# Decode step of attention and MLP, gated: two weight loads merged, the bias loaded once, the last accumulator begun four rows earlier

## The chip, the cores and the metric

The kernel runs on one core of a Trainium2 chip. The metric is the device time of one execution in microseconds (us), the median of several runs. Engines are named as in the profile: PE is TensorE's matmul, PEld its weight load, DVE is VectorE, ACT ScalarE, POOL GpSimd, SP SyncE; SPq and ACTq are the sequencers of SP and ACT, which issue the DMAs.

## The reference, cut to what matters

```python
# x [2, 1, 576], k_cache and v_cache [2, 32, 4096, 128], wq [576, 4096], wo [4096, 576],
# w1 [576, 4608], b1 [4608], w2 [4608, 576], b2 [576], gate_w [576], all float32
g = sigmoid((x * gate_w).sum(-1, keepdims=True))
q = (x @ wq).reshape(B, 1, 32, 128).transpose(0, 2, 1, 3)
p = softmax(einsum("bhqd,bhkd->bhqk", q, k_cache) * 128 ** -0.5)
a = einsum("bhqk,bhkd->bhqd", p, v_cache).transpose(0, 2, 1, 3).reshape(B, 1, 4096) @ wo
b = gelu(x @ w1 + b1) @ w2 + b2
out = g * a + (1 - g) * b
```

## The kernel before

**The ring.** One tile `ring` of 128 partitions holds everything that is loaded: three slots of 16384 floats a partition. At first wq and w1 lie in it, with small temporaries behind them (`temp`). Then 16 units pass through it, each four heads of one batch row: a K load and a V load of 8.39 MB, one slot each. Then come three last loads (`LAST`, L66 to L70), into the slots of the last-but-one V, the last K and the last V: w2's rows 0 to 27 (a "row" is one of the 36 rows of 576 floats that each partition holds), in two transfers; then w2's rows 28 to 35, a second copy of half of w2's last row spread over 16 partitions in four small transfers (`wx`), and wo's rows 0 to 15, in two transfers; then wo's rows 16 to 31, in pieces of 7, 4, 3 and 1 rows, the last row once more in three pieces. `load_last` (L143) issues these on SP, in this order; SP works through its queue in order. `load_next` (L200) issues the next load when the slot that it goes to has been named free; the instruction itself then waits for the readers of the part that it overwrites. A load also waits for an older transfer which used the same semaphore, since there are eight semaphores that are used in turn.

**The start.** `b1r` is set to zero by POOL (L210). `load_b1` (L215) puts b1 into four partitions, one in each group of 32, row 0 of the group, on ACT's queue; x and gate_w follow (L223, L224). POOL and DVE make an identity and constants (`pick` L252, `xe` L259, `xT` L272, `g1z` L372 are zeroed by DVE and then partly filled by it). PE forms x's transposes, the gate (L279) and x @ wq (`qps`, L303); ACT copies the result (L313), issues the load of b2 (L314) and, in five pieces, a second load of b1 into row 1 of each group (L315, issued at L218), and scales q (L330). `q_unit` (L343) spreads q over the partitions for four units: a multiplication on POOL (L347), a matmul (L351), a copy on ACT (L353). `acc_mm` (L363) adds a product of two rows (the two batch rows) to the accumulator `acc` in PSUM, in halves of 288 columns at one of four places; the first such product (L367) is b2's, with `g1z`. Then x @ w1 (`hps`), the addition of `b1r` (L390), a transposition (L395) and the gelu (L396 to L405), whose result times 1 - g is `hg`.

**The units.** For each unit i: `softmax` of unit i-1 (ACT, L531), then DVE multiplies K by q (L506), POOL and DVE sum over 128 (L510 to L512), DVE finds the maximum (L516 to L525); PE multiplies the probabilities of unit i-1 with V (`av`, L545).

**The end.** The order is written out by hand (L604 to L623):

```python
    softmax(k)
    mlp_out(0, 14)
    av(k)
    load_next(("v", k))
    assert not seq
    keep(k // 2)
    mlp_out(14, 18)
```

`mlp_out(lo, hi)` (L421) adds hg times w2's rows to `acc`. `keep` and `combine` (L556, L562) gather the attention's output, `norm_sum`, `norm_t` and `o_turn` (L570 to L436) divide and turn it into `oP`; between them stand further parts of `mlp_out` and `mlp_x`. `wo_out(0, FOLD)` (L438) adds oP times wo's rows below FOLD to `acc`. `last_out` (L443) copies `acc` to SBUF on ACT (L446), and gathers wo's rows from FOLD on in a second accumulator `res`, in four pieces of 144 columns a row (`part`, L457); behind the first of these rows, four matmuls with the matrix `fold` (L467) add the four places of `acc` to it. Row 31 comes in two parts, as its pieces land (L457, then L481); DVE and ACT copy the output in two steps each (L477, L486), and SP writes it (L487).

Of the kernel before, what the change touches and what calls it, by code (L numbers as in the profile page):

```python
# [12 lines left out]
P = 128  # L13
# [6 lines left out]
def kernel(  # L20
# [14 lines left out]
    nc = tc.nc  # L35
    B, H, SK, DH = k_cache.shape
# [13 lines left out]
    NG = 4  # L50
# [3 lines left out]
    F4 = F // NG  # L54
# [3 lines left out]
    NF = F // P  # L58
# [5 lines left out]
    SLOTS = 3  # L64

    LAST = (  # L66
        (("w2", 0, 14), ("w2", 14, 28)),
        (("w2", 28, 36), ("wx", 0, 1), ("wo", 0, 8), ("wo", 8, 16)),
        (("wo", 16, 23), ("wo", 23, 27), ("wo", 27, 30), ("wo", 30, 31), ("wo", 31, 32)),
    )  # L70
    FOLD = 27
    SLOT = R * DH
    ALIGN = 512
    FREE0 = 16512
# [96 lines left out]
    def temp(n, parts=P):  # L171
        t = ring[:parts, used["t"]:used["t"] + n]
        used["t"] += n
        assert used["t"] <= SLOTS * SLOT
        return t

    def late(n, parts=P):
        t = ring[:parts, used["e"]:used["e"] + n]
        used["e"] += n
        assert not seq and used["e"] <= used["z"]  # L180
        return t
# [18 lines left out]
    def load_next(what):  # L200

        free.add(what)
        while seq and held[-SLOTS] in free:
            load()
# [3 lines left out]
    b1r = temp(F4)  # L208
# [3 lines left out]
    load()  # L212
    load()

    def load_b1(b, ends):  # L215
        to, src = b1r.rearrange("(g q) n -> g q n", g=NG)[:, b], b1.rearrange("(g n) -> g n", g=NG)
        for u, v in zip(ends, ends[1:]):
            nc.scalar.dma_start(to[:, u:v], src[:, u:v])  # L218


    load_b1(0, (0, F4))
    for b in range(B):
        nc.scalar.dma_start(xg[b:b + 1], x[b])  # L223
    nc.scalar.dma_start(xg[B:B + 1], gate_w[None, :])  # L224
# [24 lines left out]
    selr = cp.tile([P, RB], F32, name="selr")  # L249
    nc.vector.tensor_reduce(selr, sel.rearrange("p j e r -> p r j e"), AX.XY, ALU.add)  # L250
    pick = cp.tile([P, 2 * NO - G], F32, name="pick")
    nc.vector.memset(pick, 0.0)  # L252
    nc.vector.tensor_reduce(pick[:, NO - G:NO], sel.rearrange("p j e r -> p e j r"), AX.XY, ALU.add)

    xe = temp(2 * P, B + 1).rearrange("p (e c) -> p e c", e=2)
    nc.vector.memset(xe, 0.0)  # L259
    for e in range(2):  # L260
        nc.vector.tensor_copy(xe[:, e, e::2], xg[:, NX * P:])  # L261
    def x_rows(rows):
# [6 lines left out]
    for c, src in enumerate(srcx):  # L269
        nc.tensor.transpose(xps[:, c, :B + 1], src, ident[:B + 1, :B + 1])  # L270
    xT = temp(NXT * 32).rearrange("p (c b) -> p c b", b=32)
    nc.vector.memset(xT, 0.0)  # L272
    nc.vector.tensor_copy(xT[:, :, :B], xps[:, :, :B])
    gT = temp(NX + 1)
    nc.vector.tensor_copy(gT, xps[:, :NX + 1, B])
# [36 lines left out]
    for m, ps in enumerate(qps):  # L312
        nc.scalar.copy(qrow[:, m * 512:(m + 1) * 512], ps)  # L313
    nc.scalar.dma_start(b2r, b2[None, :])  # L314
    load_b1(1, (0, 232, 464, 696, 928, F4))  # L315

    to = temp(HG * NO).rearrange("p (f o) -> p f o", f=HG)
# [43 lines left out]
    def acc_mm(lhsT, rhs, k, start=False, stop=False, lo=0):  # L363
        m = lhsT.shape[-1]
        for s in range(lo, lo + rhs.shape[-1] // DS):
            o = 64 * (k % 2) + 32 * s
            nc.tensor.matmul(  # L367
                acc[o:o + m], lhsT, rhs[:, (s - lo) * DS:(s - lo + 1) * DS], start=start, stop=stop, skip_group_check=True
            )

    g1z = cp.tile([1, 2, 32], F32, name="g1z")
    nc.vector.memset(g1z, 0.0)  # L372
    nc.vector.tensor_copy(g1z[:, 0, :B], g1[0:1])
    for k in range(2):
        acc_mm(g1z[:, k], b2r, k, start=True)
# [17 lines left out]

    ht = temp(F4).rearrange("p (r c) -> p r c", c=32)
    nc.vector.transpose(ht, hrow.rearrange("q (p r) -> q r p", r=NF))  # L395
    hb = ht[:, :, :B]  # L396
    hg = cp.tile([P, NF, B], F32, name="hg")
    t = temp(NF * B).rearrange("p (r b) -> p r b", b=B)
    nc.vector.tensor_mul(t, hb, hb)
# [21 lines left out]
    def mlp_out(lo, hi):  # L421
        for r in range(lo, hi):
            acc_mm(hg[:, r], rows["w2", r], r)
# [14 lines left out]
    def wo_out(lo, hi):  # L438
        for r in range(lo, hi):
            acc_mm(oP[:, :, r], rows["wo", r], r)  # L440


    def last_out():  # L443
        res = ps_big.tile([32 * (NC - 1) + B, DO], F32, tag="big", name="res")
        sums = late(DS)
        nc.scalar.copy(sums, acc)  # L446

        def half(t, s):
            if s < 2:
                return t[:, s * DO:(s + 1) * DO]  # L450
            return t.rearrange("p (q g c) -> p g q c", q=2, g=2)[:, s - 2]

        def cols(row, s):
            return half(row[:, s // 2 * DS:(s // 2 + 1) * DS], s)

        def part(r, s):
            nc.tensor.matmul(  # L457
                res[32 * s:32 * s + B], oP[:, :, r], cols(rows["wo", r], s),
                start=r == FOLD, stop=r == 31, skip_group_check=True,
            )  # L460

        for r in range(FOLD, 31):
            for s in range(NC):
                part(r, s)
            if r == FOLD:
                for s in range(NC):
                    nc.tensor.matmul(  # L467
                        res[32 * s:32 * s + B], fold[:, s // 2], half(sums, s),
                        start=False, stop=False, skip_group_check=True,
                    )  # L470

        osb = late(D, B)
        cpy = (nc.vector.tensor_copy, nc.scalar.copy)
        for s in range(2):
            part(31, s)
        for s in range(2):
            cpy[s](osb[:, s * DO:(s + 1) * DO], res[32 * s:32 * s + B])  # L477
        DW = DO // 2
        for q in range(2):
            for s in range(2, NC):  # L480
                nc.tensor.matmul(  # L481
                    res[32 * s:32 * s + B, q * DW:(q + 1) * DW], oP[:, :, 31], cols(rows["wo", 31], s)[:, q],
                    start=False, stop=True, skip_group_check=True,
                )
        for s in range(2, NC):
            cpy[s - 2](cols(osb, s), res[32 * s:32 * s + B].rearrange("p (q c) -> p q c", q=2))  # L486
        nc.sync.dma_start(out.rearrange("b s d -> (b s) d"), osb)  # L487
# [39 lines left out]
    def softmax(i):  # L527
        p = pt[i % NPB][:, EB:].rearrange("p (t c) -> p t c", c=32)
        for e in range(E):
            w = slice(e * PE_, (e + 1) * PE_)  # L530
            nc.scalar.activation(  # L531
                p[w, :, e * RB:(e + 1) * RB], st[i][w].rearrange("p (t c) -> p t c", c=RB), AF.Exp,
                bias=bias[i][w], accum_out=rs[w, i * E + e:i * E + e + 1],
            )


    def av(i):
        half = i % 2
        if half == 0:
            avs[i // 2] = ps_av.tile([P, 512], F32, tag="av", name=f"av{i // 2}")  # L540
        ps = avs[i // 2]
        p = pt[i % NPB]
        for t in range(NT):
            j = t % 4
            nc.tensor.matmul(  # L545
                ps[32 * j:32 * j + 32],
                p[:, 32 * t + EB * (1 - half):32 * t + EB * (1 - half) + 32],
                vt[i][:, RB * t:RB * (t + 1)].rearrange("p r d -> p (r d)"),
                start=(half == 0 and t < 4),
                stop=(half == 1 and t >= NT - 4),  # L550
            )


    def keep(i):
        t = ep.tile([P, RB, DH], F32, tag="avs", name=f"avs{i}")
        nc.vector.tensor_mul(  # L556
            t, avs[i].rearrange("p (r d) -> p r d", d=DH), selr.unsqueeze(2).to_broadcast([P, RB, DH])
        )
        avs[i] = t
# [43 lines left out]

    k = N - 1  # L604
    softmax(k)
    mlp_out(0, 14)
    av(k)
    load_next(("v", k))
    assert not seq
    keep(k // 2)  # L610
    mlp_out(14, 18)
    combine(k // 2)
# [8 lines left out]
    mlp_out(28, NF)  # L621
    wo_out(0, FOLD)
    last_out()  # L623


# [26 lines left out]
```

## Time and profile before

| | |
|---|---|
| time, median of 3 runs | 722.4 us (722.3 to 722.56) |
| the profiled execution: time | 722.53 us |
| the profiled execution: span | 720.5 us |
| busy: DVE, PE, POOL, ACT | 71%, 30%, 20%, 5% |
| loaded, mean rate over the span | 308.84 MB, 429 GB/s |

The span runs from the first to the last instruction of the program; the time holds some 2 us more. An engine's busy time is the sum of its instructions; DMA share is the mean busy share of the 16 DMA engines. A timeline row reads: start, duration, engine, line, operation, out<-in, shapes, count, and in brackets the idle time before and what ended it. A row of the chain of waits reads: start, duration, what. A row of a table of stretches has the length, the busy time of PE, PEld, DVE, ACT and POOL with their counts, the granted TensorE clock (1.00 is full), DMA share and GB/s.

### The profile page before, as it was taken

To read this page: it belongs to the slowest core of one execution; us is meant where nothing else is said; L and a number is where in the kernel's file an instruction comes from. 1 tells how busy PE (TensorE), PEld (TensorE's weight loads), DVE (VectorE), ACT (ScalarE), POOL (GpSimd) and SP (SyncE) were. 2 spreads that over 40 slices of the span, in tenths; PEclk is the share of its full clock that TensorE was granted. 3 is DMA by queue.
4 is the path that set the end of the run, shared out by engine and by line. 5 is a ranking of instruction groups with operands and counts; after the bars stand their busy time and mean duration, and the time that the engine had idled before them with its cause. 6 is when DMAs were issued, how large, how long until landed. Compare 5 with 4: busy or idle time off the path is not lost.

```text
span 720.5 us, 3849 instructions
## 1 busy us (share of the span) xinstructions
PE 213.3 (30%) x1631; PEld 61.1 (8%) x1631; DVE 513.9 (71%) x154; ACT 38.0 (5%) x142; POOL 144.2 (20%) x31
## 2 busy tenths in 40 slices
PE   0781022140514050504133140405060503123295
PEld 0330000010101010101000000101010101000031
DVE  0104969789695969596969879696959695978810
ACT  0010010100001010101010100001010101010100
POOL 1000130404050404022140404040503022040400
PEclk9996557565757575666656575757575665657598
DMA  9999999999999999999999999999999999999996
GB/s 409 411 446 430 426 444 415 458 416 451 422 448 427 440 426 433 434 426 440 429 438 437 437 437 433 438 426 429 440 427 437 433 438 433 440 429 441 414 421 289
DMA packets 7276, 308.84 MB, mean 429 GB/s; under 512 B 830, under 2 KB 1362, under 8 KB 1628
## 3 DMA queue, kind: packets, MB, share of 16 engines
q1 hardware_dynamic: 7204, 308.55, 99.1%
q8 instruction: 13, 0.21, 0.1%
q10 hardware_dynamic: 56, 0.05, 0.0%
q14 instruction: 3, 0.02, 0.0%
HBM read 308.59 MB, written 0.00 MB: 428 GB/s over the span
## 4 chain that ended last, share of the span: by engine, by line
DMA 49%; DVE 35%; PE 13%; ACT 2%; issue 1%; ACTq 0%; POOL 0%; DVEq 0%; SPq 0%; POOLq 0%
DMA ring<-in_A_k_cache_dram 40%; DVE ring L506 19%; DVE s L511 10%; PE av L545 9%; DVE s L512 5%; DMA ring<-in_A_wo_dram 3%; DMA ring<-in_gate_w_dram 3%; ACT p L531 2%; DMA ring<-in_B_w_dram 2%; PE hps L303 2%; PE qps L303 2%; DMA ring<-in_B_b_dram 1%; PE zps L279 0%; DVE ring L395 0%; DVE m L516 0%
## 5 line engine op out<-in xcount | busy, mean ns | idle before, releaser
L506 DVE TENSOR_TENSOR ring<-ring,q 128x16384 f32<-128x16384 f32 x16 | 275.6, 17225 | 116.4 <-DMA ring<-in_A_k_cache_dram 116.4
L510 POOL TENSOR_TENSOR ring<-ring 128x3968 f32<-128x3968 f32 x16 | 137.0, 8564 | 494.7 <-DVE ring L506 494.7
L545 PE MATMUL av<-ring,p 128*32 128x512 f32 x1024 | 138.1, 700 | 174.6 <-ACT p L531 174.6
L511 DVE TENSOR_REDUCE s<-ring 128x66 f32<-128x8448 f32 x16 | 143.2, 8953 | 1.3
L562 PE MATMUL oall<-avs,pick 128*64 128x512 f32 x16 | 14.8, 1028 | 197.0 <-DVE avs L556 169.4
L512 DVE TENSOR_REDUCE s<-ring 128x62 f32<-128x3968 f32 x16 | 68.4, 4276 | 0.0
L545 PEld LDWEIGHTS av<-ring,p 128*32 128x32 f32 x1024 | 35.3, 127 | 282.9 <-issue 218.5
L531 ACT ACTIVATE p<-s,bs 32x128 f32<-32x128 f32 x64 | 25.5, 398 | 486.1 <-DVE bs L525 484.9
L351 PE MATMUL qb<-qm,spread 64*128 64x512 f32 x8 | 7.3, 1013 | 73.2 <-POOL qm L347 73.2
L390 DVE TENSOR_TENSOR ring<-hps,ring 128x384 f32<-128x384 f32 x3 | 1.7, 559 | 26.3 <-PE hps L303 26.1
L562 PEld LDWEIGHTS oall<-avs,pick 128*64 128x64 f32 x16 | 2.2, 196 | 203.9 <-DVE avs L556 203.9
L367 PE MATMUL acc<-ring,hg 128*2 128x288 f32 x142 | 11.0, 457 | 25.4 <-DMA ring<-in_B_w_dram 25.4
L261 DVE COPY ring<-ring 3x64 f32<-3x64 f32 x2 | 0.3, 182 | 19.6 <-DMA ring<-in_gate_w_dram 19.6
L477 DVE COPY ring<-res 2x144 f32<-2x144 f32 x1 | 0.3, 297 | 17.7 <-PE res L481 17.7
L556 DVE TENSOR_TENSOR avs<-av,selr 128x512 f32<-128x512 f32 x8 | 5.5, 682 | 9.9 <-PE av L545 9.9
L531 ACT ACTIVATION_READ_ACCUMULATOR p<-s,bs 32x1 f32 x64 | 11.8, 184 | 0.0
L347 POOL TENSOR_TENSOR qm<-qall,mine 64x512 f32<-64x512 f32 x4 | 4.1, 1033 | 37.5 <-ACT qall L330 37.5
L303 PE MATMUL hps<-ring 128*32 128x384 f32 x120 | 11.5, 548 | 0.0
L367 PE MATMUL acc<-ring,oP 128*2 128x288 f32 x108 | 10.1, 505 | 4.6 <-DMA ring<-in_A_wo_dram 4.6
L303 PE MATMUL qps<-ring 128*32 128x512 f32 x80 | 11.0, 712 | 0.0
L351 PEld LDWEIGHTS qb<-qm,spread 64*128 64x128 f32 x8 | 1.8, 277 | 76.1 <-POOL qm L347 76.1
L270 PE MATMUL xps<-ident,ring 3*128 3x3 f32 x10 | 1.3, 250 | 23.0 <-DMA ring<-in_gate_w_dram 23.0
(87 smaller groups left out, 65.1 us busy)
## 6 DMA issues: line engine op xcount, KB each, us to landing
ring<-in_B_w_dram SPq DMA_DIRECT2D x2, 4608.0 KB, 34.3
ring<-in_B_w_dram SPq DMA_DIRECT2D x2, 4032.0 KB
ring<-in_A_wo_dram SPq DMA_DIRECT2D x2, 2304.0 KB, 15.2
ring<-in_B_w_dram SPq DMA_DIRECT2D x1, 2160.0 KB
ring<-in_A_wo_dram SPq DMA_DIRECT2D x1, 2016.0 KB
ring<-in_B_w_dram SPq DMA_DIRECT2D x1, 1152.0 KB, 14.6
ring<-in_A_wo_dram SPq DMA_DIRECT2D x1, 1152.0 KB
ring<-in_A_wq_dram SPq DMA_DIRECT2D x1, 1024.0 KB
```

Of the source, the lines that this page charges most:

```text
L303: nc.tensor.matmul(ps[32 * j:32 * j + 32, :width], lhs, ts[c][:, o:o + width], start=(k == 0), stop=last, skip_group_check=True,)
L347: nc.gpsimd.tensor_mul(t, qall.unsqueeze(1).to_broadcast([NO, NQ, DH]), mine[:, u[0]:u[-1] + 1].unsqueeze(2).to_broadcast([NO, NQ, DH]),)
L351: nc.tensor.matmul(ps, spread, t.rearrange("p u d -> p (u d)"), start=True, stop=True)
L367: nc.tensor.matmul(acc[o:o + m], lhsT, rhs[:, (s - lo) * DS:(s - lo + 1) * DS], start=start, stop=stop, skip_group_check=True)
L506: nc.vector.tensor_mul(kt[i], kt[i], qs[i].unsqueeze(1).to_broadcast([P, R, DH]))
L510: nc.gpsimd.tensor_add(t[:, :, :DH2], t[:, :, :DH2], t[:, :, DH2:])
L511: nc.vector.tensor_reduce(st[i][:, HALVED:], kt[i][:, HALVED:], AX.X, ALU.add)
L512: nc.vector.tensor_reduce(st[i][:, :HALVED], t[:, :, :DH2], AX.X, ALU.add)
L531: nc.scalar.activation(p[w, :, e * RB:(e + 1) * RB], st[i][w].rearrange("p (t c) -> p t c", c=RB), AF.Exp, bias=bias[i][w], accum_out=rs[w ...
L545: nc.tensor.matmul(ps[32 * j:32 * j + 32], p[:, 32 * t + EB * (1 - half):32 * t + EB * (1 - half) + 32], vt[i][:, RB * t:RB * (t + 1)].rea ...
L556: nc.vector.tensor_mul(t, avs[i].rearrange("p (r d) -> p r d", d=DH), selr.unsqueeze(2).to_broadcast([P, RB, DH]))
L562: nc.tensor.matmul(oall, pick[:, NO - G - i * G:2 * NO - G - i * G], avs[i].rearrange("p r d -> p (r d)"), start=(i == 0), stop=(i == N // ...
```

## The change

w2's rows 0 to 27 are loaded in one transfer, and so are wo's rows 0 to 15. FOLD goes from 27 to 23: wo's rows 23 to 26 go to the second accumulator, and the first one's sums are added to that after row 26. b1 is loaded once, into row 2 of each group of 32 partitions, where the product has zeros; after the transposition that row is added to the two batch rows. Four memsets move from DVE to POOL. In the last unit, `av` and the last `load_next` stand before `mlp_out(0, 14)`.

```diff
     LAST = (
-        (("w2", 0, 14), ("w2", 14, 28)),
-        (("w2", 28, 36), ("wx", 0, 1), ("wo", 0, 8), ("wo", 8, 16)),
+        (("w2", 0, 28),),
+        (("w2", 28, 36), ("wx", 0, 1), ("wo", 0, 16)),
         (("wo", 16, 23), ("wo", 23, 27), ("wo", 27, 30), ("wo", 30, 31), ("wo", 31, 32)),
     )
-    FOLD = 27
+    FOLD = 23
...
-    def load_b1(b, ends):
-        to, src = b1r.rearrange("(g q) n -> g q n", g=NG)[:, b], b1.rearrange("(g n) -> g n", g=NG)
-        for u, v in zip(ends, ends[1:]):
-            nc.scalar.dma_start(to[:, u:v], src[:, u:v])
-
-
-    load_b1(0, (0, F4))
+    nc.scalar.dma_start(b1r.rearrange("(g q) n -> g q n", g=NG)[:, B], b1.rearrange("(g n) -> g n", g=NG))
...
-    nc.vector.memset(pick, 0.0)
+    nc.gpsimd.memset(pick, 0.0)
...
-    nc.vector.memset(xe, 0.0)
+    nc.gpsimd.memset(xe, 0.0)
...
-    nc.vector.memset(xT, 0.0)
+    nc.gpsimd.memset(xT, 0.0)
...
     nc.scalar.dma_start(b2r, b2[None, :])
-    load_b1(1, (0, 232, 464, 696, 928, F4))
...
-    nc.vector.memset(g1z, 0.0)
+    nc.gpsimd.memset(g1z, 0.0)
...
-    hb = ht[:, :, :B]
+    hb = temp(NF * B).rearrange("p (r b) -> p r b", b=B)
+    nc.vector.tensor_add(hb, ht[:, :, :B], ht[:, :, B:B + 1].to_broadcast([P, NF, B]))
...
-            if r == FOLD:
+            if r == FOLD + 3:
...
     softmax(k)
-    mlp_out(0, 14)
     av(k)
     load_next(("v", k))
     assert not seq
+    mlp_out(0, 14)
     keep(k // 2)
     mlp_out(14, 18)
```

## The prediction

> **What bounds the kernel now.** I read the page's second and third parts first (which resource is full, and until when), then a table of stretches, then the tail instruction by instruction.
>
> ```profile
> span 720.5 us, 3849 instructions
> ...
> q1 hardware_dynamic: 7204, 308.55, 99.1%
> ```
>
> ```profile
> 70.00:680.00 610.00, 150.51 (x980) 36.88 (x980) 498.98 (x100) 31.18 (x123) 140.00 (x19) 0.62 1.00 434
> 680.00:700.00 20.00, 19.93 (x215) 6.74 (x219) 4.87 (x14) 1.96 (x8) 0.00 (x0) 0.92 0.99 424
> ...
> 716.00:717.00 1.00, 1.00 (x44) 0.88 (x36) 0.00 (x0) 0.00 (x0) 0.00 (x0) 1.00 0.09 28
> ```
>
> Columns of the second fence: length, busy time of PE, PEld, DVE, ACT and POOL, granted clock, DMA share, GB/s. The 16 DMA engines are full (share 0.99 to 1.00), over the span 99.1% with the tail counted in. 308.55 MB at 434 GB/s are 711 us of a 720.5 us span. So an engine saves time only if the stream runs dry for it, or if it acts after the last byte. The stream ends shortly before 717. What follows is the tail:
>
> ```profile
> 695.41 19.91 DMA ring<-in_A_wo_dram
> ```
>
> ```profile
> L166 SPq DMA_DIRECT2D ring<-in_A_wo_dram x1: 328/328/328, 700.3 to 700.3; - x1
> ...
> DMA to landing us min/median/max: 16.5/16.5/16.5
> ```
>
> ```profile
> 715.35 0.40 ACT L446 COPY ring<-acc 128x288 f32<-128x288 f32 x1 [31.01 <-PE acc L367]
> ...
> 715.37 0.43 PE L457 MATMUL res<-ring,oP 128*2 128x144 f32 x8
> ...
> 716.05 1.03 PE L457 MATMUL res<-ring,oP 128*2 128x144 f32 x26
> ...
> 716.78 0.09 PEld L457 LDWEIGHTS res<-ring,oP 128*2 128x2 f32 x2
> ...
> 716.91 0.29 PE L457 MATMUL res<-ring,oP 128*2 128x144 f32 x2
> 716.92 0.29 PE L481 MATMUL res<-ring,oP 128*2 128x72 f32 x4
> 717.23 0.30 DVE L477 COPY ring<-res 2x144 f32<-2x144 f32 x1 [17.75 <-PE res L481]
> ...
> 717.56 0.30 DVE L486 COPY ring<-res 2x144 f32<-2x144 f32 x1
> ...
> 717.92 0.29 SPq L487 DMA_DIRECT2D out_dram<-ring  x1
> ```
>
> The chain has wo's rows 27 to 29 landed at 695.41 + 19.91 = 715.32; the last piece of row 31, issued at 700.3, lands 16.5 later, at 716.8. By bytes between (288 KB of row 30; 144, 72 and 72 KB of row 31 in 1.48 us) row 30 is there at about 716.06, row 31's first piece at 716.43. PE is behind this: row 27 starts at 715.37, then PE waits for the copy of the first accumulator (715.35 to 715.75) and folds it in (eight matmuls, until 716.05); it comes to row 31 only at 716.78, 0.35 us after its first piece. The first output copy therefore starts at 717.23 and the second has to queue behind it until 717.56, though its matmuls ended at 716.92 + 0.29 = 717.21. From 717.86 on (output transfer, end: 2.6 us) nothing changes. So two things bear on the time: the stream's length, and 0.3 to 0.5 us of PE work in front of the output copies.
>
> **Part 1: start (bias, memsets).**
>
> ```profile
> 38.16 2.68 ACTq L218 DMA_DIRECT2D ring<-in_B_b_dram  x5
> ...
> 41.24 1.03 POOL L347 TENSOR_TENSOR qm<-qall,mine 64x512 f32<-64x512 f32 x1 [37.45 <-ACT qall L330]
> ...
> 44.34 0.33 SPq L130 DMA_DIRECT2D ring<-in_A_k_cache_dram  x1
> ...
> 44.39 0.70 PE L367 MATMUL acc<-ring,g1z 1*32 1x288 f32 x8 [0.94 <-DMA ring<-in_B_b_dram]
> ...
> 60.73 0.23 DVE L404 TENSOR_TENSOR ring<-ring 128x72 f32<-128x72 f32 x1
> ...
> 61.44 0.33 SPq L130 DMA_DIRECT2D ring<-in_A_k_cache_dram  x1
> ...
> 70.24 17.22 DVE L506 TENSOR_TENSOR ring<-ring,q 128x16384 f32<-128x16384 f32 x1 [8.52 <-DMA ring<-in_A_k_cache_dram]
> ```
>
> Five transfers leave ACT's queue (2.68 us of issuing), so the q row, which ACT scales behind them, and L347 come at most 2.7 us earlier. One addition of 128x72 is new on DVE, 0.23 us by L404's row, and delays the gelu and so the second K load (61.44). Neither counts. A K or V load is 8.39 MB, 19.3 us at 434 GB/s. The first K load ends at 70.2, so its bytes began at 70.2 - 19.3 = 50.9; it was issued at 44.34, and an issue at any time before 50.9 gives the same. The second K load follows the first V load, which flows until 89.5: cover 28 us. Three memsets on POOL run while it idles (37.45 us before 41.24). The fourth (g1z) stands in POOL's queue behind L347, which ended at 42.27 before; PE needs g1z at 44.39, when it waits for b2's transfer anyway. DVE's copy of g1z waits with it, and behind that copy only the fold matrix, needed at 715. A memset of these shapes on POOL isn't shown; 0 and L347's 1.03 us for 64x512 bound it, I take the latter, and 2.1 us of cover take it. Loads on SP also wait for older transfers in turn, and five fewer shift which one; the first K load needs only to go before 50.9. Sum: 0. If the cover went, each us of a dry stream would cost a us.
>
> **Part 2: merged transfers (stream).** No row shows a 64 KB row of w2 against two of 32 KB.
>
> ```profile
> 700.30:703.70 3.40, 2.90 (x47) 1.01 (x38) 0.00 (x0) 0.00 (x0) 0.00 (x0) 1.00 1.01 432
> ```
>
> Here rows of 18 KB (wo, 8 rows of 576 floats) move: 432 / 1.01 = 428 GB/s per full share, against 434 with the 64 KB rows of K and V. That is 1.4% of the 0.68 us that 18432 bytes take at 27.1 B/ns, 9.5 ns for each row. The merges take away 8 + 8 rows from each DMA engine: 0.15 us. The bias transfers were 18 KB, 0.04 us, beside it. Ends: 0, and 0.7 us if the 13 MB concerned went at 434 in place of 424. I take 0.15, off the landing of everything behind; the nearest rows give it.
>
> The Trainium skill ("DMA: Bandwidth & Descriptors", section "Anatomy of one DMA") gives a transfer a fixed cost of about 2.0 us beside its bytes. By that, two transfers less in SP's stream would be up to 4 us; what that gives here is a rival below.
>
> **Part 3: order and PE before the tail.** The w2 load now waits until all of V14's slot is read, 3.4 us later than its first half did:
>
> ```profile
> 651.33 3.76 SPq L166 DMA_DIRECT2D ring<-in_B_w_dram  x2
> ...
> 680.07 5.11 PE L367 MATMUL acc<-ring,hg 128*2 128x288 f32 x56 [25.38 <-DMA ring<-in_B_w_dram]
> ...
> 684.16 0.18 ACT L531 ACTIVATION_READ_ACCUMULATOR p<-s,bs 32x1 f32 x1
> ...
> 685.01 7.04 PE L545 MATMUL av<-ring,p 128*32 128x512 f32 x64
> ...
> 694.01 2.61 PE L367 MATMUL acc<-ring,hg 128*2 128x288 f32 x40
> ```
>
> ```profile
> 606.09 9.80 PE av L545 x64
> ```
>
> Half of w2 (0 to 14, 4.13 MB, 9.5 us) landed at 680.07, so its bytes began at 670.5; issuing at 655.1 is 15 us early. It is complete at 680.07 + 9.5 = 689.6, less 0.08.
> The last av no longer has 56 matmuls ahead of it. It can start at 684.4 (softmax ends 684.34) but on a cold clock, so as in the loop: at most 9.80 us, end 694.2 (before 692.05). Behind it come the 56 matmuls, w2 being there: 40 took 2.61 us, the last one's own 0.4 us included, so 0.057 us each, 3.2 us. PE is 2.1 + 3.2 = 5.3 us later than before. SP's last seven loads wait for this av alone (V15's slot), not for the 56 matmuls; they need to go before wo's rows 0 to 15 have landed, 705.6: 11 us of cover.
>
> ```profile
> 700.62 0.41 PE L367 MATMUL acc<-ring,oP 128*2 128x288 f32 x1
> ...
> 705.81 2.79 PE L367 MATMUL acc<-ring,oP 128*2 128x288 f32 x32 [2.60 <-DMA ring<-in_A_wo_dram]
> 710.57 4.73 PE L367 MATMUL acc<-ring,oP 128*2 128x288 f32 x44 [1.97 <-DMA ring<-in_A_wo_dram]
> ...
> 713.31 0.25 PEld L367 LDWEIGHTS acc<-ring,oP 128*2 128x2 f32 x6 [0.24 <-DMA ring<-in_A_wo_dram]
> ```
>
> wo's first rows then start at 700.62 + 5.3 = 705.9, and 64 matmuls of 0.057 us end at 709.6. Rows 16 to 22 land at 710.4 (0.15 earlier than the row at 710.57): 28 matmuls, 1.6 us, drained at 712.4. PE is idle three times, about 0.8 us each, before the tail: 2.4 us of delay would be taken up.
>
> **Part 4: FOLD 23.** The sums are copied at 712.4 to 712.8. Rows 23 to 26 (landed 713.15) take 32 matmuls of half the width: 26 such took 1.03 us, the last one's 0.29 included, 0.03 us each, so 0.96 us, as much as the 16 wide ones. The eight of the fold (0.25 us) follow, done by 714.4. In the tail: rows 27 to 29 land at 715.17, 24 matmuls end at 715.94; row 30 (there at 715.91) ends at 716.18; row 31's first piece is there at 716.28 and, like before (716.78 to 717.20), needs 0.42: first copy 716.77 to 717.07. The last piece lands at 716.65 and, as before, ends its matmuls 0.41 later, 717.06; second copy 717.10 to 717.40, against 717.86: **0.46 us less**, 0.15 of it the stream's and 0.31 PE's.
>
> Sum: 0 + 0.46. The profiled execution took 722.53 us (span 720.5 and 2.0 around it), 0.13 over the median of 722.4; taken from the median: **721.94 us**.
>
> **Rivals.**
> *PE's part is hidden anyway:* the last piece sets the end, or PE isn't ahead by 716.28; only the stream's 0.15 or nothing stays: 722.25 to 722.4. For it: the last matmuls start within 0.1 us of the last landing already.
>
> *Cold tail (slower).* The clock is granted by stretches:
>
> ```profile
> 652.50:655.90 3.40, 2.20 (x24) 0.36 (x12) 3.40 (x1) 0.00 (x0) 0.00 (x0) 1.00 1.05 448
> 655.90:659.33 3.43, 0.00 (x0) 0.00 (x0) 3.43 (x1) 0.00 (x0) 0.00 (x0) 1.00 1.06 459
> ```
>
> ```profile
> 703.70:707.10 3.40, 1.29 (x24) 0.60 (x28) 0.00 (x0) 0.00 (x0) 0.00 (x0) 1.00 0.99 416
> 707.10:710.50 3.40, 1.50 (x16) 0.19 (x8) 0.00 (x0) 0.00 (x0) 0.00 (x0) 0.50 0.98 418
> 710.50:713.95 3.45, 3.38 (x32) 1.13 (x36) 0.00 (x0) 0.00 (x0) 0.00 (x0) 0.50 0.98 404
> ```
>
> A stretch with PE busy 2.20 of 3.40 us kept the clock; one with 1.29 of 3.40 lost it for the next. Before, the cold stretch to 713.95 kept PE busy, and the tail was warm. After, a stretch from 711.9 to 715.3 would hold two idle gaps and be busy for about 1.6 of 3.4, between the two. Below the deciding share, rows 27 to 31 run at half speed: four rows 2.0 us from 715.2, row 31 twice 0.42 from 717.2, copies until 718.6, 0.7 us over before: 723.1. The stretches' phase has to hit this within some 0.3 of 3.4 us.
> The Trainium skill ("TensorE: Matmul & The Clock Gate", section "What's actually happening") has the clock fall after an idle window of about 3.4 us. By it this rival can't occur, the gaps being 0.8 us; the row at 703.70 (1.29 us busy, clock lost) speaks against so mild a reading.
>
> *Dry stream (slower):* SP's seven loads issued after 705.6, each us a us; held to 708 it is 724.8. Against it: 11 us of cover.
>
> *A fixed cost for each transfer:* 2 us for each of two merged transfers, 718.4. Against it: from 680 to 713.95, where one transfer follows another, the rows have the share at 0.98 to 1.01, so no such gap stands between them.
>
> **How the numbers follow.** Forecast 0.70, hidden 0.17, cold tail 0.08, dry stream 0.03, fixed cost 0.02. Range 721.4 (0.7 in place of 0.15 from the stream) to 722.6 (the hidden case with the 0.2 us that the three runs differ); outside it the cold tail, the dry stream and the fixed cost, 0.13. A measurement of this kernel tells apart about 0.2%, 1.4 us: faster 0.03 (fixed cost, 0.01 of the forecast), slower 0.04 (dry stream, a worse cold tail), same 0.93.
>
> **What would show it.** After: DMA share unbroken to about 716.7; av of the last head ahead of w2's matmuls, ending by 694.2; the accumulator's copy at 712 to 713, the fold done before 715; L457 for row 31 starting 0.4 us earlier; copies L477 and L486 no longer queued at 717.56. Wrong: a clock of 0.5 in 713 to 717, PE still in wo's rows 0 to 15 after 712, or a DMA share below 0.9 in any stretch before 713.

## The result and the profile after

The changed kernel takes **724.12 us** (median of 14 runs, 723.62 to 725.23), the kernel before 722.56 us on the same chip (14 runs, 722.3 to 722.78). The ratio is 1.0023, with a 95% interval of 1.0016 to 1.0031. So the change costs 1.6 us, where 0.46 us less was forecast, and the time lies outside the forecast's range of 721.4 to 722.6. The profiled execution took 723.93 us.

The page of the changed kernel, the two lines that answer to the first of before:

```profile
span 721.8 us, 3870 instructions
...
q1 hardware_dynamic: 6916, 308.55, 99.0%
```

The bytes are the same, and the span is 1.3 us longer. The stream no longer runs through, and a table of stretches finds the place; columns as before (length, busy PE, PEld, DVE, ACT, POOL, clock, DMA share, GB/s):

```profile
690.00:695.00 5.00, 5.00 (x64) 1.80 (x60) 0.99 (x2) 0.00 (x0) 0.00 (x0) 1.00 0.92 325
695.00:700.00 5.00, 5.00 (x76) 2.08 (x68) 0.91 (x3) 0.00 (x0) 0.00 (x0) 1.00 0.88 372
...
690.00:691.00 1.00, 1.00 (x16) 0.37 (x12) 0.00 (x0) 0.00 (x0) 0.00 (x0) 1.00 1.05 449
691.00:692.00 1.00, 1.00 (x15) 0.27 (x8) 0.00 (x0) 0.00 (x0) 0.00 (x0) 1.00 0.65 273
692.00:693.00 1.00, 1.00 (x16) 0.30 (x12) 0.00 (x0) 0.00 (x0) 0.00 (x0) 1.00 0.55 202
693.00:694.00 1.00, 1.00 (x20) 0.41 (x16) 0.35 (x1) 0.00 (x0) 0.00 (x0) 1.00 0.71 212
694.00:695.00 1.00, 1.00 (x24) 0.44 (x16) 0.64 (x2) 0.00 (x0) 0.00 (x0) 1.00 1.64 491
```

From 691 to 694 the DMA share falls to 0.55 to 0.71, although all 9.4 MB of wo are still to come. (A packet is one DMA engine's piece of a load. A row counts each packet whole, in the stretch in which it starts; so the last row comes to 1.64, more than the engines can be busy, and single rows are rough.) What was issued, and when, is in SP's timeline (start, duration, line, transfer, count). First the kernel before, then the changed one, then the one row of the changed kernel's waits that explains the difference (who waited, for what; us in total, times, longest):

```profile
681.43 0.33 SPq L158 DMA_DIRECT2D ring<-in_B_w_dram  x1
682.19 2.84 SPq L155 DMA_DIRECT2D ring<-in_B_w_dram  x4
685.07 15.54 SPq L166 DMA_DIRECT2D ring<-in_A_wo_dram  x9
```

```profile
681.60 0.33 SPq L158 DMA_DIRECT2D ring<-in_B_w_dram  x1
689.96 2.83 SPq L155 DMA_DIRECT2D ring<-in_B_w_dram  x4
692.83 4.20 SPq L166 DMA_DIRECT2D ring<-in_A_wo_dram  x8
```

```profile
SPq L155 <- DMA ring<-in_B_w_dram: 7.6, 1, 7.6
```

L158 issues w2's rows 28 to 35, L155 the four small wx loads, L166 all of wo. After the change the first wx load waits 7.6 us for a transfer of w2. wo's nine (now eight) loads stand behind it in SP's queue, and the first of them goes out at 692.83 in place of 685.07. Until then only L158's 2.21 MB and wx stand behind the merged load, and part of these had moved beside its last rows: from 690 to 694 packets of no more than 449 + 273 + 202 + 212 = 1136 KB start, 2.6 us of work at 434 GB/s. The Trainium skill ("DMA: Bandwidth & Descriptors", section "Anatomy of one DMA") says that DMA engines don't wait on semaphores: a wait happens on the issuing sequencer, before dispatch. The trace agrees: SP holds everything behind wx for these 7.6 us, and no engine works ahead on wo.

The end, as a chain of waits (start, duration, what) and as a timeline:

```profile
681.60 13.02 DMA ring<-in_B_w_dram
...
694.69 22.67 DMA ring<-in_A_wo_dram
...
717.40 1.48 PE res L451 x36
```

```profile
707.77 4.06 PE L360 MATMUL acc<-ring,oP 128*2 128x288 f32 x64 [1.57 <-DMA ring<-in_A_wo_dram]
712.44 2.11 PE L360 MATMUL acc<-ring,oP 128*2 128x288 f32 x28 [0.61 <-DMA ring<-in_A_wo_dram]
714.59 0.40 ACT L440 COPY ring<-acc 128x288 f32<-128x288 f32 x1 [30.09 <-PE acc L360]
...
717.40 1.48 PE L451 MATMUL res<-ring,oP 128*2 128x144 f32 x36 [0.69 <-DMA ring<-in_A_wo_dram]
718.91 0.30 DVE L471 COPY ring<-res 2x144 f32<-2x144 f32 x1 [14.50 <-PE res L475]
719.24 0.30 DVE L480 COPY ring<-res 2x144 f32<-2x144 f32 x1
719.61 0.29 SPq L481 DMA_DIRECT2D out_dram<-ring  x1
```

wo's rows 27 to 29 land at 694.69 + 22.67 = 717.36; before it was 715.32. The stream ends 2.04 us later. Behind that landing the output is issued after 719.61 - 717.36 = 2.25 us; before, after 717.92 - 715.32 = 2.60. So the end of the work on PE became 0.35 us shorter, as forecast. 2.04 - 0.35 = 1.69, against 1.6 in the medians and 1.4 between the two profiled executions.

The single packets in the trace account for the 2.04 us. wo's first packets start at 693.91, 1.1 us after their issue, and between 691 and 695 a DMA engine is idle for 1.3 us in the mean. Then the first packet of wo on most engines takes 1.6 to 2.4 us, where later ones take 1.36; that is another 0.7 us for each engine.

### The profile page after: what moved, and what is told of

Same layout as the page of the kernel before. It is cut to its first block, busy times and chain, and to the rows that moved or that the text cites. A ratio compares the mean times of both kernels' runs of the same rounds, so it can differ in the third digit from the quotient of the medians.

```text
span 721.8 us, 3870 instructions
## 1 busy us (share of the span) xinstructions
PE 211.1 (29%) x1647; PEld 61.7 (9%) x1647; DVE 513.5 (71%) x151; ACT 37.9 (5%) x142; POOL 145.0 (20%) x35
## 4 chain that ended last, share of the span: by engine, by line
DMA 49%; DVE 35%; PE 13%; ACT 2%; issue 1%; ACTq 0%; DVEq 0%; POOL 0%; SPq 0%; POOLq 0%
DMA ring<-in_A_k_cache_dram 40%; DVE ring L500 19%; DVE s L505 10%; PE av L539 9%; DVE s L506 5%; DMA ring<-in_A_wo_dram 3%; DMA ring<-in_gate_w_dram 3%; ACT p L525 2%; DMA ring<-in_B_w_dram 2%; PE hps L297 2%; PE qps L297 1%; DMA ring<-in_B_b_dram 1%; PE zps L273 0%; DVE ring L388 0%; DVE m L510 0%
## 5 line engine op out<-in xcount | busy, mean ns | idle before, releaser
L539 PE MATMUL av<-ring,p 128*32 128x512 f32 x1024 | 140.1, 709 | 206.3 <-ACT p L525 206.3
L360 PE MATMUL acc<-ring,hg 128*2 128x288 f32 x142 | 9.3, 406 | 0.0
```

What stands on the lines that cost most here:

```text
L360: nc.tensor.matmul(acc[o:o + m], lhsT, rhs[:, (s - lo) * DS:(s - lo + 1) * DS], start=start, stop=stop, skip_group_check=True)
L539: nc.tensor.matmul(ps[32 * j:32 * j + 32], p[:, 32 * t + EB * (1 - half):32 * t + EB * (1 - half) + 32], vt[i][:, RB * t:RB * (t + 1)].rea ...
```

## The experiments

**The theories.** A: the load into every fourth partition of the ring (`xt[c::XC]`) comes upon a wait for the landing of the merged w2 transfer, though it writes other bytes; with two transfers of 14 rows it does not. Everything behind it in SP's queue is late, and the stream runs dry. B: the merged transfer with its 64 KB rows is itself slower, or lands later, and the wait is a symptom. C: another part of the change (start, FOLD, order) costs the time. Each version ran beside the kernel before; intervals are 95%.

**1. w2 in two transfers again, all else of the change kept.**

```diff
-        (("w2", 0, 28),),
+        (("w2", 0, 14), ("w2", 14, 28)),
```

> The changed kernel with one part undone: w2's rows 0 to 27 are again two transfers. Theory A (the first of the four small wx transfers now waits on SP until the merged w2 transfer has landed, wo's first load stands behind it, and the DMA engines run dry at 691 to 694.5): the wait goes, the stream is unbroken, wx issues at about 682, and what stays is PE's part and the merged wo: 722.1 to 722.3 against 722.56 before. Rival B (64512-byte rows of the merged transfer are slow in themselves): the same, 722.3, so this run doesn't part A from B. Rival C (the last av ahead of w2's matmuls makes PE late, or the start costs): nothing changes, 724.1.

722.12 us (721.77 to 722.56), the kernel before beside it 722.48; ratio 0.9996 (0.9986 to 1.0005). The loss is gone. wx is issued at once:

```profile
682.29 2.84 SPq L155 DMA_DIRECT2D ring<-in_B_w_dram  x4
685.17 11.84 SPq L166 DMA_DIRECT2D ring<-in_A_wo_dram  x8
```

So w2's merge carries the loss, and C falls. A and B are both still open.

**2. w2 merged; wx in neighbouring partitions.** The four loads write the same 16 partitions, each four neighbours in place of every fourth. Their number, bytes and place in the queue stay.

```diff
-    srcx2 = w2.rearrange("(e c s r) n -> c r e s n", ...)[:, NF - 1, :, :, DS:]
+    srcx2 = w2.rearrange("(e c s r) n -> e r c s n", ...)[:, NF - 1, :, :, DS:]
...
-                for c in range(XC):
-                    nc.sync.dma_start(xt[c::XC]..., srcx2[c])
+                for e in range(XE):
+                    nc.sync.dma_start(xt[e * XC:(e + 1) * XC]..., srcx2[e])
```

> The changed kernel, all of its parts kept; only the four small wx transfers write four neighbouring partitions each instead of every fourth one, the same bytes to the same places. Their instructions then name no wait. Theory A: 722.0 to 722.2, the first wx issue at 682, the DMA share unbroken to 716.7. Rival B: 724.1, w2's landing late. Rival C: 724.1 with an unbroken stream.

721.93 us (721.51 to 722.15), 0.07 under what was expected; ratio to before 0.9991 (0.9982 to 1.0). That is 2.19 us less than the changed kernel, and A is borne out against B: the merged transfer with its long rows is still there, and costs nothing. Since the loads keep their number and order, the turn of the eight semaphores is excluded as the cause too. SP's timeline, the stretches and the chain of this version:

```profile
681.98 3.26 SPq L155 DMA_DIRECT2D ring<-in_B_w_dram  x4
685.28 11.61 SPq L166 DMA_DIRECT2D ring<-in_A_wo_dram  x8
```

```profile
690.00:695.00 5.00, 5.00 (x64) 1.77 (x60) 0.88 (x2) 0.00 (x0) 0.00 (x0) 1.00 1.06 445
695.00:700.00 5.00, 5.00 (x75) 2.07 (x68) 1.14 (x4) 0.00 (x0) 0.00 (x0) 1.00 1.06 453
```

```profile
694.67 20.64 DMA ring<-in_A_wo_dram
```

From 690 to 700 the changed kernel moved (445 - 325 + 453 - 372) x 5 = 1005 KB less than this one by these rows; at 434 GB/s that is 2.3 us, roughly the delay of the landing: wo's rows 27 to 29 land at 715.31 here against 717.36: 2.05 us.

**3. The kernel before, with w2's merge alone.**

```diff
-        (("w2", 0, 14), ("w2", 14, 28)),
+        (("w2", 0, 28),),
```

> The kernel before with one part of the change: w2's rows 0 to 27 in one transfer. Theory A: wx's first issue at 689.5 to 690, wo's behind it, the last landing 2.0 us later, as in the changed kernel, and PE, which here takes w2's 14 rows ahead of av and so starts them 9.5 us later, is late as well: 724.5 to 725.5. Rival B: w2's landing is late, the issue of wx at 682: 723 to 724. Rival C (order): 722.6 plus what PE's delay costs, at most 723.5, with an unbroken stream.

725.59 us (725.15 to 726.16); ratio 1.0044 (1.0031 to 1.0056), a little over what was expected. Here the old order shows when the merged load lands:

```profile
689.49 5.95 PE L367 MATMUL acc<-ring,hg 128*2 128x288 f32 x56 [34.29 <-DMA ring<-in_B_w_dram]
...
689.91 2.84 SPq L155 DMA_DIRECT2D ring<-in_B_w_dram  x4
```

PE has w2's rows at 689.49, and wx goes out 0.4 us later: the wait ends with the merged load's landing. PE is also late in this version, since the head's last av stands behind those 56 matmuls and the loads of the final rows behind the av. In the chain of waits PE sets the end from 709.48 on:

```profile
709.48 8.47 PE acc L367 x135
```

So the 3.1 us hold both, the late loads and the late PE, and aren't parted here.

**4. The kernel before, with FOLD alone** (27 to 23, the fold behind row 26).

> The kernel before with one part of the change: FOLD 23, the first accumulator's sums added after row 26. The prediction's part 4 has PE's gain there, 0.31 us: rows 16 to 22 end their cold matmuls at about 714.0, the copy ends at 714.8, the fold is done by 715.3, and the second output copy starts 0.3 us earlier: 722.25. Rival (the 32 half-wide matmuls cost PE more than the 16 wide ones, and PE is late for row 27): 722.6 to 722.9.

722.26 us (722.0 to 722.46); ratio 0.9996 (0.9988 to 1.0005). That fits a gain of 0.2 us and fits none; a loss of 1 us is excluded. The end is the forecast one:

```profile
715.43 1.52 PE L457 MATMUL res<-ring,oP 128*2 128x144 f32 x36
...
717.67 0.29 SPq L487 DMA_DIRECT2D out_dram<-ring  x1
```

**5. The kernel before, with the start alone** (b1 once, memsets on POOL).

> The kernel before with the start's part of the change alone: b1 loaded once and added after the transposition, four memsets on POOL. The prediction's part 1 has 0: K's first load issues anywhere before 50.9, the rest is covered: 722.4 to 722.6. A rival that the first runs leave room for: part of what the changed kernel's other parts gain comes from here (less small packets in the stream), 722.2 to 722.3; or the start costs, 722.8.

722.33 us (722.13 to 722.8), the kernel before beside it 722.52; ratio 0.9999 (0.999 to 1.0008): nothing that can be told from 0, as forecast.

**6. The changed kernel, wx as it was, but behind wo's rows 0 to 15 in SP's queue.** The wait is kept, and should hold up nobody. `mlp_x` comes later too.

```diff
-        (("w2", 28, 36), ("wx", 0, 1), ("wo", 0, 16)),
+        (("w2", 28, 36), ("wo", 0, 16), ("wx", 0, 1)),
...
-    mlp_x()
     o_turn(turn)
     mlp_out(28, NF)
-    wo_out(0, FOLD)
+    wo_out(0, 16)
+    mlp_x()
+    wo_out(16, FOLD)
```

> The changed kernel, with wx as it writes there (the wait on w2's merged transfer stays), but placed behind wo's rows 0 to 15 in SP's queue; its product on PE moves behind those rows too. Theory A says that not the wait costs but what is queued behind it: wo's rows 0 to 15 issue at about 682, wx at 689.5 to 693 while 4.7 MB of wo are still to come, the DMA share stays at 1 and the last landing is at 716.7: 722.0 to 722.3. Rival (the wait itself, or a transfer of 64512-byte rows, slows the stream): 723.5 to 724.1.

727.08 us (726.95 to 728.49); ratio 1.007 (1.0057 to 1.0082). The expectation missed by 5 us. Half of it came true: wo's first load went out at 682.07, ahead of wx, and the stream ran through:

```profile
690.00:695.00 5.00, 5.00 (x57) 1.57 (x52) 0.48 (x1) 0.00 (x0) 0.00 (x0) 0.99 1.08 463
695.00:700.00 5.00, 5.00 (x72) 2.12 (x68) 0.21 (x1) 0.00 (x0) 0.00 (x0) 1.00 1.02 438
...
716.00:717.00 1.00, 1.00 (x12) 0.33 (x8) 0.00 (x0) 0.00 (x0) 0.00 (x0) 1.00 0.06 18
```

But the same loads brought a second wait, on the attention's way to `oP`. First the chain of waits, then DVE's timeline:

```profile
691.84 13.24 DMA ring<-in_B_w_dram
```

```profile
705.10 0.28 DVE L608 COPY ring<-ident 128x128 f32<-128x128 f32 x1 [9.89 <-DMA ring<-in_B_w_dram]
```

This copy writes `turn`, which lies in the ring behind the loads. It waited for the last wx load itself, which was issued at 691.84 and landed 13.24 us later, behind wo's first rows; and the normalisation of the attention stood behind the copy on DVE. In the kernel before the same copy had such a wait too, 1.81 us long, and nothing that set the end hung on it:

```profile
694.63 0.29 DVE L614 COPY ring<-ident 128x128 f32<-128x128 f32 x1 [1.81 <-DMA ring<-in_B_w_dram]
```

Moving wx made it 9.89 us, PE came late, and the second output copy began at 722.20 (717.56 before).

**7. Version 2 with `mlp_out(0, 14)` ahead of `av(k)` again.**

> The second run's kernel (all parts of the change, wx in neighbouring partitions, no wait) with the order undone: w2's rows 0 to 13 ahead of the last av on PE. The stream is then unbroken and PE alone is late: it waits for w2 until 689.4, av ends at about 702 as in the run with the merge alone, wo's products start at 710.9 and run without a gap to the end, the last copies 1.5 to 2 us later than before: 723.9 to 724.5. Rival (the order is worth nothing, the slack of 2.4 us takes the delay up): 721.9 to 722.1.

724.67 us (723.84 to 725.18), a little over what was expected; ratio 1.0029 (1.0017 to 1.004). With w2 in one transfer the new order is needed: PE stands still until the whole of it has landed, and the last av comes behind.

```profile
689.54 5.24 PE L360 MATMUL acc<-ring,hg 128*2 128x288 f32 x56 [35.07 <-DMA ring<-in_B_w_dram]
694.61 7.04 PE L539 MATMUL av<-ring,p 128*32 128x512 f32 x64
```

**8. The kernel before, with wx in neighbouring partitions alone.**

> Control: the kernel before, only with wx's four transfers writing four neighbouring partitions each. If the second run's gain over the changed kernel was the wait's alone, nothing happens here, since the wait that wx has before (on the last V load) ends at 670.5, long before SP comes to it: 722.4 to 722.6. If the layout itself were faster, 722.0 to 722.2.

722.85 us (722.55 to 723.47), 0.25 over what was expected; ratio 1.0006 (0.9997 to 1.0015), so no difference from the kernel before can be told. The layout has no gain of its own, so what version 2 wins back is the wait.

**9. Version 6 with wx in neighbouring partitions.** It asks whether the 727.08 came from the place in the queue or from the same kind of wait.

> The changed kernel with wx behind wo's rows 0 to 15 in SP's queue, as in the run that came out at 727.08, and with wx's four loads each into four neighbouring partitions in place of every fourth. Nothing is left out. Theory A (the instruction that comes upon a load into every fourth partition names more transfers than the ones whose bytes it needs; there it was DVE's copy of the matrix turn, 9.89 us late): the neighbouring partitions take that wait from DVE too, and the time is that of the version with wx in its old place, 721.9 to 722.3. Rival (the place behind wo costs the time, since wx lands late whatever it writes): about 727 again, with DVE's copy at 705.

721.82 us (721.53 to 722.23), 0.08 under what was expected, the kernel before beside it 722.49; ratio 0.9992 (0.9983 to 1.0001).

```profile
693.70 0.33 DVE L608 COPY ring<-ident 128x128 f32<-128x128 f32 x1
```

DVE's copy no longer waits, with wx in the same late place: in the trace its packets run from 702.95 to 705.36, long after the copy. So it was the wait. This and version 2 are the two fastest, 721.82 and 721.93; their ranges overlap, and either lies some 2.2 us under the changed kernel and 0.6 us under the kernel before.

## Why the prediction was wrong, point by point

**What bounds the kernel: right.** The stream sets the end, and an engine or a queue costs time where it lets the stream run dry. That is just what happened, at another place than was looked at.

**Part 1, the start: right.** The first K load is issued 9 us earlier and DVE starts on it at the same time (70.24 before):

```profile
35.41 0.33 SPq L130 DMA_DIRECT2D ring<-in_A_k_cache_dram  x1
...
70.22 17.23 DVE L500 TENSOR_TENSOR ring<-ring,q 128x16384 f32<-128x16384 f32 x1 [9.74 <-DMA ring<-in_A_k_cache_dram]
```

The start alone came out at 0.9999 of before (version 5).

**Part 2, the merged rows: too small to be told.** Version 2 has w2 in one transfer and version 1 in two: 721.93 and 722.12, with ranges that overlap. In the single profiles wo's rows 27 to 29 land at 715.31 in version 2 and 715.32 before, so the 0.15 us isn't to be seen there either. The rival of a fixed cost falls: 2 us for a transfer would stand out between versions 1 and 2. The Trainium skill's 2.0 us ("DMA: Bandwidth & Descriptors", section "Anatomy of one DMA") is given there for transfers that GpSimd issues; these are issued by SP. It is not added where transfers are queued behind each other, as versions 1 and 2 show. Where the queue ran empty some delay is seen: in the changed kernel wo's first load is issued at 692.83, and its first packets start at 693.91.

**Part 3: the step that failed.** "SP's last seven loads wait for this av alone (V15's slot), not for the 56 matmuls; they need to go before wo's rows 0 to 15 have landed, 705.6: 11 us of cover." This asks when the last loads may go, and took for granted that the loads ahead of them go as before, at 682.19 and 685.07. wx, with its load into every fourth partition, stands between the merged transfer and all of wo, and its wait was not asked for. The same part asked of w2 only when it may be issued ("15 us early", and so it was), not who waits for its landing, which the merge moves from 680.07, for the first half, to 689.5 for all of it. "11 us of cover" was beside the point, since the stream broke ahead of those loads: when w2's merged load had landed at 689.5, some 1230 KB of rows 28 to 35 and wx's 147 KB were still to move, 3.2 us of work at 434 GB/s, and the first of wo moved 4.4 us later, at 693.91. The sum has no term for this; the runs put 2.05 us there (wo's rows 27 to 29 land at 717.36 in the changed kernel, at 715.31 in version 2). One of the prediction's own signs of being wrong, a DMA share below 0.9 before 713, is the one that came.
The rest of this part held. av ran from 684.60 for 8.98 us, to 693.58 (forecast: by 694.2). In version 2, where nothing holds the stream, PE begins wo's rows at 705.93 (forecast 705.9), and ends them at 709.99 (709.6):

```profile
705.93 4.06 PE L360 MATMUL acc<-ring,oP 128*2 128x288 f32 x64
710.59 2.11 PE L360 MATMUL acc<-ring,oP 128*2 128x288 f32 x28 [0.59 <-DMA ring<-in_A_wo_dram]
712.74 0.40 ACT L440 COPY ring<-acc 128x288 f32<-128x288 f32 x1 [28.22 <-PE acc L360]
714.29 0.43 PE L461 MATMUL res<-ring,fold 128*2 128x144 f32 x8
715.36 1.45 PE L451 MATMUL res<-ring,oP 128*2 128x144 f32 x36 [0.63 <-DMA ring<-in_A_wo_dram]
...
717.17 0.30 DVE L480 COPY ring<-res 2x144 f32<-2x144 f32 x1
```

**Part 4, FOLD: right.** In the same rows the sums are copied at 712.74 (forecast 712.4), the fold is done at 714.72, ahead of row 27, and the second output copy runs from 717.17 to 717.47 (717.10 to 717.40). The changed kernel has this gain too, 0.35 us behind a landing that is 2.04 us late.

**The rivals.** *Dry stream* (0.03) was right in kind. Its place was wrong: it looked for a dry stream after 705.6, by the seven last loads, and the stream ran dry at 691, by wx. *Cold tail* did not come. The row of version 2 for the stretch that was feared has the clock at 1.00:

```profile
711.90:715.30 3.40, 2.21 (x52) 1.05 (x42) 0.00 (x0) 0.40 (x1) 0.00 (x0) 1.00 0.83 329
```

PE is busy for 2.21 of the 3.40 us there, not 1.6 as the rival had it, and 2.20 had kept the clock before too. *Hidden anyway* falls by the profile: the 0.35 us behind the last landing are there.

**What stays open.** That the loads into every fourth partition bring SP's wait is shown by version 2 against the changed kernel, and that they bring DVE's by version 9 against version 6. SP's costs time with w2 in one transfer and not with two (version 1). Whether it is there with two is not shown: a wait for the first of them, landed at 680.07 before SP came to wx at 682.19, would not be seen, and only a wait for the second is excluded. DVE's is there with two transfers as well (1.81 us before). Why either wait names transfers of other bytes was not tried. Whether FOLD, the start and the merges win 0.2 us each or nothing can't be told from these runs; only their sum, 0.6 us in versions 2 and 9, shows in the medians, and its intervals reach 1.0.

## What to carry to other kernels

Where transfers are merged, ask not only when the larger one may start, but which instruction waits for its landing, and what stands behind that instruction in its queue: the price is the time for which the queue has nothing to give to the DMA engines, and here about half of that again until the stream was back at its rate. A small load with a stride over partitions, in a tile that many loads share, is the first to look at: its waits can name transfers whose bytes it doesn't touch, and the same wait may sit on other engines that write the tile. A forecast that checks the last loads of a queue has to walk through each load ahead of them too.

## What the runs showed of the hardware

The wait is the program's, not the chip's: a wait instruction stands in SP's queue ahead of the wx loads in the changed kernel and in versions 3 and 6, and none in versions 2 and 9. The row of the changed kernel (line, engine, operation, count, ns, start):

```profile
L155 SPq EVENT_SEMAPHORE  x1: 17/17/17, 689.5 to 689.5; - x1
```

Of the chip: when the queue had run empty, the rate came back only some time after the next issue. wo's first load went out at 692.83, its first packets started at 693.91, and the first one on most engines took 1.6 to 2.4 us, where later ones took 1.36. In version 3, with packets half as long, it was 692.79, 693.86, and 1.0 to 1.7 us against 0.69. So here the queue had to be filled more than a us before it was empty. And the stretch of version 2 with PE busy for 2.21 of 3.40 us, with gaps of 0.6 us, kept the full clock.
